# Block-sparse attention before a feed-forward layer: masked dense tiles replaced by gathered key and value blocks

## The chip, the cores and the metric

One NeuronCore of a Trainium2 chip runs the whole program. The metric is device time in microseconds (us), the median over the executions of a kernel. Engines are called PE (TensorE; PEld is its weight load), ACT (ScalarE), DVE (VectorE), POOL (GpSimd) and SP (SyncE, which here only issues DMA). PEclk is the clock that the throttle granted to TensorE, as a share of full speed. PV is the product of the exponentials with V; of the two operands of a matmul, the one that PEld loads is called stationary here, the other moving. A run is called slow when it took over 1.5% longer than the fastest of the same kernel, else fast; a single run alone is of unknown state. A call is a set of runs made together on one chip.

## The reference, cut to what matters

```python
# q, k, v: [4, 8, 768, 64] float32; blocks of 32 rows, 24 blocks; 3 sampled blocks a query block
mask = np.abs(blk_i - blk_j) <= 1                        # neighbours
mask = mask | (blk_i == 0) | (blk_j == 0) | (blk_i == 23) | (blk_j == 23)
for qb in range(24):
    for kb in sampled_blocks[qb]: mask[rows(qb), rows(kb)] = True
attn = softmax(where(mask, q @ k.T / 8, -1e9));  x = attn @ v   # -> [3072, 512]
h = x @ w_in                       # 512 -> 1024
solu = h * softmax(h)
out = layernorm(solu) * g_ln @ w_out                     # 1024 -> 512
```

A middle query block needs at most 8 of 24 key blocks: two ends, itself and two neighbours, three sampled.

## The kernel before: the parts that matter

It computes all 24 key blocks and adds the mask through extra contraction rows. Work goes by batch, query tile of 256 rows (`t`) and head pair. The three tiles of a batch are finished one after the other, so the feed-forward layer (FFN) of tile 0 starts after four short units, and one FFN tile is left over at the end.

```python
def transpose_pair(b, pr):                 # K and Q of two heads
    for src, dst in ((kc, kT[i]), (qc, qT[i])):
        tp = ps_m.tile([P, S], BF16, ...)  # PSUM
        for c in range(NCH):
            nc.tensor.matmul(tp[:, c*P:(c+1)*P], src[:, c, :, :], ident, is_transpose=True, ...)
        nc.vector.tensor_copy(out=dst[0:D, 0, pr, :], in_=tp[0:D, :])   # dense, L165
        nc.vector.tensor_copy(out=dst[D:P, 1, pr, :], in_=tp[D:P, :])   # dense, L166
# ... cut ...
units = [(b, t, pr) for b in range(B) for t in range(NT) for pr in range(NPR)]
for u, (b, t, pr) in enumerate(units):
    for n in range(3):
        scores(b, t, pr, n, exs)           # 4 matmuls of 256 columns, one Exp of 128x1024
        if n == 0 and prev is not None:
            pv(...)                        # 24 matmuls, 128 stationary columns, 65 moving
            if ppr == NPR - 1: bg.extend(ffn_pieces(...))
        if bg: bg.popleft()()              # one piece of an FFN tile between score groups
# in the FFN, the layer norm's row statistics run on POOL (L293 to L298 here):
#   mul, add, sub, pow(-0.5), each 128x2 or 128x4; the output scaling waits for the last
```

The softmax here doesn't subtract the row's maximum and nothing guards it: scores larger than these inputs give would overflow.

Of the kernel before, what the change touches and what calls it, by code (L numbers as in the profile page):

```python
# [10 lines left out]
I32 = mybir.dt.int32  # L11
AX = mybir.AxisListType
# [6 lines left out]
def kernel(  # L19
# [11 lines left out]
    nc = tc.nc  # L31
# [3 lines left out]
    NB = S // BLK  # L35
    NR = sampled_blocks.shape[1]
    P = 128
    NCH = S // P
    NT = 3
    TW = 2 * P  # L40
    NPR = H // 2
    NEG = -30000.0
# [8 lines left out]
    ld = ctx.enter_context(tc.tile_pool(name="ld", bufs=3))  # L51
    vpool = ctx.enter_context(tc.tile_pool(name="vpool", bufs=2))
    expp = ctx.enter_context(tc.tile_pool(name="expp", bufs=8))
# [6 lines left out]

    kT = [const.tile([P, 2, NPR, S], BF16, name=f"kT{i}") for i in range(2)]
    qT = [const.tile([P, 2, NPR, S], BF16, name=f"qT{i}") for i in range(2)]
    for t in (kT[0], qT[0]):
        nc.vector.memset(t[0:D, 1, 0, :], 0.0)
    va = [const.tile([P, H, NCH, D + 1], BF16, name=f"va{i}") for i in range(2)]


    def load_pair(b, pr):
        got = []
        for src, nm in ((k, "kc"), (q, "qc")):  # L70
            t = ld.tile([P, NCH, 2, D], BF16, tag=nm, name=nm)
            for hh in range(2):
                nc.gpsimd.dma_start(  # L73
                    out=t[:, :, hh, :],
                    in_=src[b, 2 * pr + hh, :, :].rearrange("(p c) d -> p c d", p=P))
            got.append(t)
        t = ld.tile([P, 2, NCH, D], BF16, tag="vc", name="vc")
        nc.gpsimd.dma_start(
            out=t.rearrange("p h c d -> p h (c d)"),
            in_=v[b, 2 * pr : 2 * pr + 2, :, :].rearrange("h (p c) d -> p h (c d)", p=P))  # L80
        got.append(t)
        return got

    loaded = {}
    loaded[(0, 0)] = load_pair(0, 0)


    ident = const.tile([P, P], BF16, name="ident")
    nc.vector.memset(ident, 0.0)
    nc.gpsimd.affine_select(out=ident, in_=ident, compare_op=ALU.not_equal,  # L90
                            fill=1.0, base=0, channel_multiplier=1,
                            pattern=[[-1, P]])

    maskT = const.tile([NB, NB], FP32, name="maskT")
    nc.vector.memset(maskT, 0.0)
    for base, cm, pat, fill in ((1, -1, [[1, NB]], NEG), (1, 1, [[-1, NB]], NEG),
                                (-1, 1, [[0, NB]], 0.0), (NB - 2, -1, [[0, NB]], 0.0),
                                (-1, 0, [[1, NB]], 0.0), (NB - 2, 0, [[-1, NB]], 0.0)):
        nc.gpsimd.affine_select(out=maskT, in_=maskT, compare_op=ALU.is_ge,
                                fill=fill, base=base, channel_multiplier=cm,  # L100
                                pattern=pat)
    _t = sampled_blocks.tensor
    _t32 = bass.DRamTensorHandle(_t.name, (2 * NB * NR,), I32)
    samp_i = const.tile([1, NB * NR, 2], I32, name="samp_i")
    nc.sync.dma_start(out=samp_i.rearrange("a b c -> a (b c)"),
                      in_=bass.AP(tensor=_t32, offset=0, ap=[[0, 1], [1, 2 * NB * NR]]))
    ones1 = const.tile([1, NB], BF16, name="ones1")
    nc.vector.memset(ones1, 1.0)
    samp_lo = const.tile([1, NB * NR], BF16, name="samp_lo")
    nc.vector.tensor_copy(out=samp_lo, in_=samp_i[:, :, 0])  # L110
    samp_ps = ps_m.tile([NB, NB, NR], FP32, tag="m", name="samp_ps")
    nc.tensor.matmul(samp_ps.rearrange("a b c -> a (b c)"), ones1, samp_lo,
                     start=True, stop=True)
    kb_iota_i = const.tile([NB, 1], I32, name="kb_iota_i")
    nc.gpsimd.iota(kb_iota_i, pattern=[[0, 1]], base=0, channel_multiplier=1)
    kb_iota = const.tile([NB, 1], FP32, name="kb_iota")
    nc.vector.tensor_copy(out=kb_iota, in_=kb_iota_i)
    eq = const.tile([NB, NB, NR], FP32, name="eq")
    nc.vector.tensor_scalar(out=eq, in0=samp_ps, scalar1=kb_iota, scalar2=None,
                            op0=ALU.is_equal)  # L120
    anyeq = const.tile([NB, NB], FP32, name="anyeq")
    nc.vector.tensor_reduce(out=anyeq, in_=eq, axis=AX.X, op=ALU.max)
    nc.vector.tensor_scalar(out=anyeq, in0=anyeq, scalar1=-1.0, scalar2=1.0,
                            op0=ALU.mult, op1=ALU.add)
    nc.vector.tensor_mul(out=maskT, in0=maskT, in1=anyeq)
    sel = const.tile([NB, NB, BLK], BF16, name="sel")
    nc.vector.memset(sel, 0.0)
    nc.gpsimd.affine_select(out=sel, in_=sel, compare_op=ALU.not_equal,
                            fill=1.0, base=0, channel_multiplier=1,
                            pattern=[[-1, NB], [0, BLK]])  # L130
    mskb = const.tile([NB, NB, BLK], BF16, name="mskb")
    nc.vector.tensor_copy(
        out=mskb, in_=maskT.rearrange("p (q o) -> p q o", o=1).broadcast_to([NB, NB, BLK]))

    selp = const.tile([NB, 1, S], BF16, name="selp")
    mskp = const.tile([NB, 1, S], BF16, name="mskp")
    for dst, src in ((selp, sel), (mskp, mskb)):
        nc.vector.tensor_copy(
            out=dst.rearrange("b o (c p) -> b (o c) p", c=NCH),
            in_=src.rearrange("b n o -> b (n o)").rearrange("b (p c) -> b c p", c=NCH))  # L140
# [3 lines left out]
    def put_mask_rows(i, p0, p1):  # L144
        for hh, r0 in ((0, D), (1, 0)):
            for dst, src in ((kT, selp), (qT, mskp)):
                for p in range(p0, p1):
                    nc.sync.dma_start(out=dst[i][r0 : r0 + NB, hh, p, :],
                                      in_=src[:, 0, :])

    for hh, r0 in ((0, D), (1, 0)):
        for dst, src in ((kT, selp), (qT, mskp)):
            nc.vector.tensor_copy(out=dst[0][r0 : r0 + NB, hh, 0, :], in_=src[:, 0, :])

    def transpose_pair(b, pr):
        i = b % 2
        kc, qc, vc = loaded.pop((b, pr))
        for src, dst in ((kc, kT[i]), (qc, qT[i])):
            tp = ps_m.tile([P, S], BF16, tag="m", name="tp")
            for c in range(NCH):  # L160
                nc.tensor.matmul(tp[:, c * P : (c + 1) * P],  # L161
                                 src[:, c, :, :], ident,
                                 is_transpose=True, start=(c == 0),
                                 stop=(c == NCH - 1))
            nc.vector.tensor_copy(out=dst[0:D, 0, pr, :], in_=tp[0:D, :])  # L165
            nc.vector.tensor_copy(out=dst[D:P, 1, pr, :], in_=tp[D:P, :])  # L166
        nc.vector.tensor_copy(out=va[i][:, 2 * pr : 2 * pr + 2, :, 0:D],
                              in_=vc)
# [3 lines left out]
    w_out_f = const.tile([P, KF, d_model], FP32, name="w_out_f")  # L172
    w_out_g = const.tile([P, KF, d_model], BF16, name="w_out_g")
# [5 lines left out]
    neg_half = const.tile([P, 2], FP32, name="neg_half")  # L179

    def load_weights():
        nc.gpsimd.dma_start(out=w_in_sb, in_=moe_w_in.rearrange("(c p) f -> p c f", p=P))
        nc.sync.dma_start(out=g_sb, in_=moe_g_ln.rearrange("(c p) -> p c", p=P))
        nc.sync.dma_start(out=w_out_f, in_=moe_w_out.rearrange("(c p) d -> p c d", p=P))
        nc.vector.memset(onesf, 1.0)
        nc.vector.memset(neg_half, -0.5)
        nc.vector.memset(st_sel, 1.0 / d_ff)
        nc.vector.memset(st_sel[:, :, 0:1], eps_ln ** 0.5)

    def prep_w1():  # L190
        for c in range(KF):
            nc.vector.tensor_scalar(out=w_out_g[:, c, :], in0=w_out_f[:, c, :],
                                    scalar1=g_sb[:, c : c + 1], scalar2=None,
                                    op0=ALU.mult)

    def prep_w2():
        cs = ps_m.tile([P, d_model], FP32, tag="m", name="cs")
        for c in range(KF):
            nc.tensor.matmul(cs, onesf, w_out_g[:, c, :], start=(c == 0),
                             stop=(c == KF - 1))  # L200
        nc.scalar.mul(out=wbar, in_=cs, mul=1.0 / d_ff)
        for c in range(KF):
            nc.vector.scalar_tensor_tensor(  # L203
                out=w_out_sb[:, c, :], in0=w_out_f[:, c, :], scalar=g_sb[:, c : c + 1],
# [3 lines left out]
    rows = (slice(0, D + NB), slice(0, P))  # L208

    def scores(b, t, pr, n, exs):  # L210
        i = b % 2
        s = ps_s.tile([P, 4, TW], FP32, tag="s", name="s")
        for m in range(4):
            hh, jc = divmod(4 * n + m, NCH)
            nc.tensor.matmul(s[:, m, :],  # L215
# [108 lines left out]
    for pr in range(1, NPR):  # L324
        loaded[(0, pr)] = load_pair(0, pr)
        if pr == 1:
            load_weights()
# [79 lines left out]
```

## Time and profile before

The median was 282.56 us (two runs, 282.11 to 283.0).

| | busy us | share |
|---|---|---|
| PE | 238.8 | 85% |
| ACT | 174.4 | 62% |
| DVE | 157.9 | 56% |
| POOL | 82.8 | 29% |

The page of the kernel before: busy time, DMA traffic, then the chain of work that ended last, by engine and by line.

```profile
span 281.1 us, 7445 instructions
...
PE 238.8 (85%) x3163; PEld 183.2 (65%) x3177; DVE 157.9 (56%) x365; ACT 174.4 (62%) x206; POOL 82.8 (29%) x142
...
DMA packets 61636, 20.40 MB, mean 73 GB/s; under 512 B 52225, under 2 KB 56994, under 8 KB 61602
...
PE 62%; DMA 11%; ACT 10%; DVE 9%; issue 3%; POOL 3%; ACTq 0%; POOLq 0%
```

PE is busy most of the span and is 62% of the chain: it is the bound.

The same kernel by stretches: until the first FFN matmul, until the last PV matmul, and the rest. Columns: the stretch, its length, busy us of PE, PEld, DVE, ACT and POOL (count), PEclk, DMA share and GB/s.

```profile
0.00:52.00 52.00, 24.09 (x242) 17.78 (x244) 34.41 (x79) 17.94 (x19) 34.28 (x53) 1.00 1.42 169
52.00:266.00 214.00, 205.52 (x2825) 159.42 (x2833) 117.18 (x274) 153.35 (x183) 47.24 (x85) 1.00 0.39 52
266.00:281.00 15.00, 9.17 (x99) 6.02 (x101) 6.27 (x13) 3.08 (x5) 1.27 (x4) 0.94 0.10 36
```

In the middle PE works 205.5 of 214 us at full clock.

The timeline of the kernel before, one burst of PV matmuls (start, length, engine, line, operation, count):

```profile
112.38 0.91 PE L231 MATMUL op<-va_92,ex 128*128 128x65 bf16 x24
```

### The profile page before, as it was taken

The numbers are of one execution on the slowest core, as the hardware profiler recorded it, in microseconds if no ns is written. First come the engines' busy times: TensorE is split into PE (matmuls) and PEld (weight loads), VectorE is DVE, ScalarE is ACT, GpSimd is POOL, SyncE is SP. The second block draws the span as 40 slices with busy tenths as digits, with TensorE's granted clock in tenths as the row PEclk, the third lists the DMA queues.
The fourth block names the chain that finished last, engine by engine and source line by source line (L and its number), as shares of the span: only waits on it lengthen the run. The fifth ranks groups of instructions, "written<-read, shape, count | busy, mean of one in ns | idle before, by whom it ended". The sixth has DMA issues, their size and how long they took to land.

```text
span 281.1 us, 7445 instructions
## 1 busy us (share of the span) xinstructions
PE 238.8 (85%) x3163; PEld 183.2 (65%) x3177; DVE 157.9 (56%) x365; ACT 174.4 (62%) x206; POOL 82.8 (29%) x142
## 2 busy tenths in 40 slices
PE   0116686999999999999999999999999999899783
PEld 0004564867867867867767768678678577686561
DVE  3079789648639622756666616386376236155261
ACT  1002468548858859667677688588488595785630
POOL 8695861218139110045253100140100101001001
PEclk9999999999999999999999999999999999999998
DMA  5999999409759810049279020090100200200202
GB/s 117 264 191 188 185 180 118 58 4 140 48 93 128 85 54 23 2 90 100 30 109 79 3 77 2 37 96 2 47 31 2 77 2 2 76 2 3 76 0 77
DMA packets 61636, 20.40 MB, mean 73 GB/s; under 512 B 52225, under 2 KB 56994, under 8 KB 61602
## 3 DMA queue, kind: packets, MB, share of 16 engines
q0 software_dynamic: 55056, 10.49, 45.8%
q1 hardware_dynamic: 6546, 9.43, 9.8%
q8 instruction: 25, 0.41, 0.6%
q14 instruction: 9, 0.07, 0.1%
HBM read 23.07 MB, written 6.29 MB: 104 GB/s over the span
## 4 chain that ended last, share of the span: by engine, by line
PE 62%; DMA 11%; ACT 10%; DVE 9%; issue 3%; POOL 3%; ACTq 0%; POOLq 0%
PE s L215 15%; PE h L268 15%; PE ops L304 14%; PE op L231 10%; ACT ex L220 8%; DMA kc<-in_k_dram 7%; PE s3p L283 6%; DMA vc<-in_v_dram 4%; DVE w_out_sb L203 2%; ACT ot L312 2%; PE tp L161 2%; POOL qc L73 1%; DVE xT L258 1%; PE tps L256 1%; DVE x L240 1%
## 5 line engine op out<-in xcount | busy, mean ns | idle before, releaser
L220 ACT ACTIVATE ex<-s 128x1024 bf16<-128x1024 f32 x144 | 141.1, 1024 | 68.9 <-PE s L215 67.8
L215 PE MATMUL s<-qT_87,kT_85 88*128 88x256 bf16 (+1 forms) x288 | 49.5, 284 | 5.8 <-ACT ex L220 3.1
L231 PEld LDWEIGHTS <-ex 128*128 128x128 bf16 x1152 | 45.7, 98 | 11.1 <-ACT ex L220 4.6
L268 PE MATMUL h<-xT,w_in_sb 128*128 128x256 bf16 x384 | 47.8, 272 | 1.3 <-DVE xT L258 0.6
L215 PE MATMUL s<-qT_88,kT_86 88*128 88x256 bf16 (+1 forms) x288 | 46.2, 272 | 2.0 <-ACT ex L220 1.2
L273 DVE TENSOR_TENSOR solu<-h,e 128x512 bf16<-128x512 f32 x48 | 33.0, 687 | 26.3 <-ACT e L272 26.2
L304 PE MATMUL ops<-w_out_sb,solu 128*128 128x512 bf16 x179 | 44.6, 378 | 0.9 <-DVE s_4734 L290 0.3
L268 PEld LDWEIGHTS <-w_in_sb 128*128 128x128 bf16 x384 | 37.0, 97 | 6.3 <-issue 1.6
L272 ACT ACTIVATE e<-h 128x512 bf16<-128x512 f32 x48 | 28.7, 598 | 18.1 <-PE h L268 16.9
L215 PEld LDWEIGHTS <-kT_85 88*128 88x128 bf16 (+1 forms) x288 | 27.3, 101 | 13.5 <-issue 6.0
L73 POOL DMA_DIRECT2D kc<-in_k_dram x32 | 26.8, 841 | 18.6 <-PE tp L161 17.7
L215 PEld LDWEIGHTS <-kT_86 88*128 88x128 bf16 (+1 forms) x288 | 26.0, 97 | 9.3 <-issue 4.0
L304 PEld LDWEIGHTS <-solu 128*128 128x128 bf16 x192 | 18.4, 97 | 18.1 <-issue 0.3
L73 POOL DMA_DIRECT2D qc<-in_q_dram x32 | 26.2, 822 | 8.0 <-DMA w_in_sb<-in_moe_w_in_dram 3.7
L231 PE MATMUL op<-va_92,ex 128*128 128x65 bf16 x576 | 26.2, 193 | 2.7 <-ACT ex L220 2.2
L231 PE MATMUL op<-va_91,ex 128*128 128x65 bf16 x576 | 25.2, 196 | 1.9 <-DVE x L240 1.0
L239 DVE RECIPROCAL r<-op 128x4 f32<-128x4 f32 x48 | 8.5, 180 | 30.8 <-PE op L231 29.3
L274 DVE TENSOR_TENSOR sq<-solu 128x512 bf16<-128x512 bf16 x48 | 20.4, 425 | 1.3
L240 DVE TENSOR_TENSOR x<-op,r 128x256 bf16<-128x256 f32 x48 | 20.1, 420 | 1.0
L161 PE MATMUL tp<-ident,kc 128*128 128x128 bf16 x96 | 9.2, 240 | 12.2 <-DMA kc<-in_k_dram 10.5
L309 DVE TENSOR_SCALAR ot<-ops,rs 128x512 f32<-128x512 f32 x12 | 9.0, 751 | 16.7 <-PE ops L304 12.7
L312 ACT ACTIVATE ot<-ops,rs 128x512 f32<-128x512 f32 x12 | 8.2, 687 | 14.3 <-PE ops L304 14.3
(127 smaller groups left out, 201.7 us busy)
## 6 DMA issues: line engine op xcount, KB each, us to landing
out_dram<-ot SPq DMA_DIRECT2D x24, 256.0 KB
kc<-in_k_dram POOLq DMA_DIRECT2D x32, 96.0 KB, 5.1
qc<-in_q_dram POOLq DMA_DIRECT2D x32, 96.0 KB, 4.4
vc<-in_v_dram POOLq DMA_DIRECT2D x16, 192.0 KB, 5.0
w_out_f<-in_moe_w_out_dram SPq DMA_DIRECT2D x1, 2048.0 KB
w_in_sb<-in_moe_w_in_dram POOLq DMA_DIRECT2D x1, 1024.0 KB, 9.5
kT_86<-selp SPq DMA_DIRECT2D x8, 36.0 KB
qT_88<-mskp SPq DMA_DIRECT2D x8, 36.0 KB
```

The costliest lines, as they stand in the source:

```text
L73: nc.gpsimd.dma_start(out=t[:, :, hh, :], in_=src[b, 2 * pr + hh, :, :].rearrange("(p c) d -> p c d", p=P))
L161: nc.tensor.matmul(tp[:, c * P : (c + 1) * P], src[:, c, :, :], ident, is_transpose=True, start=(c == 0), stop=(c == NCH - 1))
L215: nc.tensor.matmul(s[:, m, :], kT[i][rows[hh], hh, pr, jc * P : (jc + 1) * P], qT[i][rows[hh], hh, pr, t * TW : (t + 1) * TW], start=(m % ...
L220: nc.scalar.activation(out=e, in_=s, func=ACT.Exp, scale=scale)
L231: nc.tensor.matmul(op[:, qt, hh, :], exs[n][:, m, qt * P : (qt + 1) * P], va[i][:, 2 * pr + hh, jc, :], start=first, stop=(n == 2 and m == ...
L240: nc.vector.tensor_tensor(out=x[:, :, 2 * pr * D : (2 * pr + 2) * D].rearrange("p a (h d) -> p a h d", h=2), in0=op[:, :, :, 0:D], in1=r.b ...
L268: nc.tensor.matmul(h[:, ff, :], w_in_sb[:, c, f * P : (f + 1) * P], st["xT"][:, c, :], start=(ff == 0 and c == 0), stop=(ff == 1 and c == ...
L272: nc.scalar.activation(out=st["e"][:, sl, :], in_=h, func=ACT.Exp)
L273: nc.vector.tensor_mul(out=st["solu"][:, sl, :], in0=h, in1=st["e"][:, sl, :])
L274: nc.vector.tensor_mul(out=st["sq"][:, sl, :], in0=st["solu"][:, sl, :], in1=st["solu"][:, sl, :])
L283: nc.tensor.matmul(s3p[:, qt, g : g + 1], st[nm][:, f, qt * P : (qt + 1) * P], onesf[:, 0:1], start=first, stop=(qt == 1 and g == 2 and f ...
L304: nc.tensor.matmul(ops, st["solu"][:, f, qt * P : (qt + 1) * P], w_out_sb[:, f, :], start=(f == 0), stop=(f == KF - 1))
```

## The change

The intent is to compute only what the mask lets through. The scores of a head pair shrink from 9,216 PE columns to 3,584, and so does the exp on ACT. The price is data movement:

- K^T of a pair is copied to SBUF (`kT`); end and neighbour blocks are grouped by two DVE copies (`kg`); sampled blocks are gathered by POOL (`krt`, two indirect copies a pair).
- V is cast, written to a scratch in DRAM, read back in two layouts, and its sampled rows are gathered by 22 indirect DMAs a batch.
- Q^T is written block-diagonally (`qbd`), so that one matmul scores both heads.
- A unit is now a head pair over all 768 queries; the FFN of a batch starts after four pairs, and three FFN tiles of the last batch come at the end.

The core of the diff, cut:

```diff
-        nc.vector.tensor_copy(out=dst[0:D, 0, pr, :], in_=tp[0:D, :])
-        nc.vector.tensor_copy(out=dst[D:P, 1, pr, :], in_=tp[D:P, :])
+        tp = ps_m.tile([P, R8, PL], BF16, ...)          # R8 = 8 residues, PL = 96; key row = 8*a + r
+        for r in range(R8): nc.tensor.matmul(tp[:, r, :], kr[:, r, :, :], perm, is_transpose=True, ...)
+        nc.scalar.copy(out=kT.rearrange("p (a r) -> p r a", r=R8), in_=tp)              # L262
+        nc.vector.tensor_copy(out=kg[:, :, 1, :], in_=kT[:, 0 : NM * BLK]...)           # and ends, L266
+        for l in range(2):
+            nc.gpsimd.indirect_copy(krt[:, l*NL:(l+1)*NL, :], kT.bitcast(U32)..., kidx[:, l, 0:NLC], True)
+        for hh, eng in ((0, nc.scalar.copy), (1, nc.vector.tensor_copy)):               # L287
+            eng(out=dst[sl, :, hh, :].rearrange("p t (a r) -> p r t a", r=R8),
+                in_=tp[sl].rearrange("p r (t a) -> p r t a", t=NCH))
+    nc.sync.dma_start(out=v_s[b][0:S, :]..., in_=vst...)         # V round trip; v0, vn read back
+    nc.gpsimd.indirect_dma_start(out=t[:, i, :], in_=v_s[b][:, :], in_offset=...vidx...)   # 22 a batch
+    # scores: 17 matmuls of 128 columns and 22 of 64; PV: 64 or 32 stationary columns
-    units = [(b, t, pr) ...]
+    for n in range(N + 1):  b, pr = divmod(n, NPR)  ...
+        if i == 3 and ppr == NPR - 1:
+            for t in range(NT): bg.extend(ffn_pieces(pb, t, xs[pb]))
```

## The prediction

> **What bounds the kernel now.** TensorE. The page's busy table gives PE 239 of 281 us (85%), ACT 174, DVE 158, POOL 83; by stretches of 20 us, PE is 19.0 to 19.6 busy from 60 to 240 us, ACT only about 14.3. The chain of waits is 62% PE. One FFN tile is exposed at the end (about 266 to 279 us).
>
> From bursts in the timeline: a 256-column matmul costs about 107 ns, a 512-column one 214, a 128-column one 55, a 65-column PV matmul about 31. So PE needs: scores 576 x 107 = 62 us, PV 1152 x 31 = 36, FFN about 101 (h 41, ops 41, sums 13, transposes 5), K/Q transposes 11. Sum about 210.
>
> **What the change does.**
> - Scores: 147,456 columns become 57,344. Exp on ACT (144 x 1.02 = 141 us) falls to about 59. ACT gains the K^T and half of the Q^T copies, about 1.6 us a pair, 26 in all: 174 -> about 120.
> - PE scores: per pair 17 of 128 columns and 22 of 64, 1.65 us: 62 -> 26 us.
> - PV matmuls do not fall: 1152 -> 1248, now with 64 or 32 stationary columns. [...] Estimate 3.3 to 4.5 us a pair: 36 -> 53 to 72 us.
> - So PE is nearly unchanged: about 190 to 210 us. ACT was not the limit; most of its saving is worth nothing.
> - DVE: fp32 casts of K, Q, V and copies for grouped keys replace the transposed-tile copies. Estimate about 10 us a pair with FFN, 165 to 190 in all.
> - POOL: 32 indirect copies of 704 words and 88 indirect DMAs (a plain issue takes 0.82 us; I take 1.1). The copy's price is unknown[...]. I take 2.5. POOL total: 80 + 97 + 20, about 200 us.
>
> **The schedule.** V goes load, cast, DRAM, gather before the first PV: estimate PV of pair 0 at 35 to 48 us. Pairs 2 and 3 follow at about 9 us. FFN starts only after four pairs (about 66 us). Twelve pairs with three quarters of an FFN tile each cost PE about 12.6 us, 13.5 with waits: to about 228. Then three FFN tiles of the last batch are exposed instead of one, about 12 us each (the exposed tile before took about 13): 264 to 268.
>
> Prediction: 268 us, range 238 to 315. Faster by over 2%: 0.60; within: 0.13; slower: 0.27.
>
> **What would show it.** ACT busy about 120; score matmuls about 26 us of PE spacing; PV bursts of 24 narrow matmuls longer than the 0.91 us of 24 full ones; PE busy share lower than 85%; POOL about 200 with indirect copies near 2.5 us.
>
> **What would make it wrong.** Indirect copies at 5 us or gathers at over 1.5: POOL becomes the limit (over 17 us a pair), 300 to 340 us. Narrow PV matmuls as cheap as 31 ns or running side by side, and POOL out of the way: pairs of 11 us, about 240. A longer start (SP's in-order waits), or DVE lag stalling PE on the two-buffer PSUM pool, adds 10 to 30.

Two terms stay as my estimates, which no trace of the kernel before shows: 53 to 72 us of PE for PV, and 2.5 us for an indirect copy. The 5 us is a limit, not a measured price. PE is 26 + 53 to 72 + 101 + 11, about 190 to 210 us, and POOL is 80 (32 x 2.5) + 97 (88 x 1.1) + 20, about 200 us.

## More of the kernel before

DMA moves 20.4 MB.

The groups of instructions of the kernel before (by line; busy us, mean ns of one, then idle time before them and what ended it):

```profile
L220 ACT ACTIVATE ex<-s 128x1024 bf16<-128x1024 f32 x144 | 141.1, 1024 | 68.9 <-PE s L215 67.8
...
L166 DVE COPY kT_86<-tp 64x768 bf16<-64x768 bf16 x8 | 4.5, 561 | 0.1
```

The copy that takes a transposed tile out of PSUM costs 561 ns for 768 columns.

## The result and the profile after

The changed kernel took 464.07 us (463.91 and 464.22) against 282.56: 1.642 times the time, 95% interval 1.631 to 1.654. A ratio here is the mean time of one kernel's fast runs over that of the other's of the same rounds, so it is not quite the ratio of the medians. The output was correct. The prediction of 268 us, range 238 to 315, was wrong by far.

The page of the changed kernel:

```profile
span 462.1 us, 7827 instructions
...
PE 243.5 (53%) x3366; PEld 179.6 (39%) x3384; DVE 213.3 (46%) x362; ACT 201.3 (44%) x158; POOL 144.7 (31%) x181
...
DMA packets 35930, 52.86 MB, mean 114 GB/s; under 512 B 4276, under 2 KB 19256, under 8 KB 35896
...
ACT 23%; PE 21%; issue 17%; DVE 13%; POOL 12%; DMA 9%; another core or an unknown queue 3%; SPq 1%; ACTq 0%; POOLq 0%
ACT kT L262 10%; POOL vr L238 9%; PE h L441 7%; PE ops L477 4%; PE s L315 4%; ACT qbd_179 L287 4%; ACT qbd_180 L287 4%; DVE qbd_179 L287 3%; DVE qbd_180 L287 3%; DMA kc<-in_k_dram 3%; DMA v_240<-v_s_173 2%; PE op L354 2%; POOL krt L271 2%; PE s3p L456 2%
```

No engine is over 53% busy, and the chain is spread over all of them: the kernel is bound by waits. The copies `kT` and `qbd` out of the transposed tile are 24% of the chain (10+4+4+3+3). DMA moves 2.6 times the bytes.

Groups of the changed kernel:

```profile
L271 POOL INDIRECT_COPY krt<-kT,kidx 128x704 uint32 x32 | 40.7, 1273 | 184.4 <-issue 124.5
...
L262 ACT COPY kT<-tp 128x768 bf16<-128x768 bf16 x16 | 57.2, 3572 | 18.2 <-PE tp L259 18.2
...
L485 ACT ACTIVATE ot<-ops,rs 128x512 f32<-128x512 f32 x12 | 8.2, 687 | 96.4 <-POOL rs L471 27.5
...
L287 ACT COPY qbd_179<-tp 64x768 bf16<-64x768 bf16 x8 | 29.0, 3619 | 23.4 <-PE tp L282 23.4
L287 DVE COPY qbd_180<-tp 64x768 bf16<-64x768 bf16 x8 | 28.5, 3557 | 20.6 <-ACT qbd_180 L287 20.6
...
L482 DVE TENSOR_SCALAR ot<-ops,rs 128x512 f32<-128x512 f32 x12 | 9.0, 751 | 44.1 <-POOL rs L471 38.9
```

Each copy out of `tp` takes 3.56 to 3.62 us, where the kernel before took 0.56 for as many columns. On 16 pairs they are 57 us for `kT`, 58 for ACT's half of `qbd` and 57 for DVE's. The last number of DVE's `qbd` line says that DVE waited for ACT's half: the two halves run one after the other. The two `ot` lines are waits for POOL's `rs`, 27.5 and 38.9 us.

A stretch of the timeline of the changed kernel, one pair (lines of other engines left out; in brackets, idle time before and what ended it):

```profile
288.80 3.60 ACT L287 COPY qbd_180<-tp 64x768 bf16<-64x768 bf16 x1
...
292.42 3.55 DVE L287 COPY qbd_180<-tp 64x768 bf16<-64x768 bf16 x1 [0.70 <-ACT qbd_180 L287]
...
296.03 0.30 PE L456 MATMUL s3p<-onesf,e 128*128 128x1 bf16 x6 [4.69 <-DVE qbd_180 L287]
...
299.29 3.58 ACT L262 COPY kT<-tp 128x768 bf16<-128x768 bf16 x1
...
304.86 0.52 PE L354 MATMUL op<-vr,e_2813 128*32 128x65 bf16 x24
```

PE stands still for 4.69 us until DVE has finished the second half. The last line answers to the PV burst of before: 24 matmuls with 32 stationary columns take 0.52 us here, less than the 0.91 us of 24 full ones.

Another stretch, POOL alone:

```profile
226.16 1.70 POOL L271 INDIRECT_COPY krt<-kT,kidx 128x704 uint32 x1 [24.97 <-ACT e_2248 L321]
229.94 1.20 POOL L271 INDIRECT_COPY krt<-kT,kidx 128x704 uint32 x1 [2.08 <-issue]
231.30 1.29 POOL L238 DMA_INDIRECT vr<-v_s_175,vidx  x1 [0.17 <-issue]
232.90 0.96 POOL L238 DMA_INDIRECT vr<-v_s_175,vidx  x1 [0.30 <-issue]
...
245.44 0.95 POOL L238 DMA_INDIRECT vr<-v_s_175,vidx  x1 [0.30 <-issue]
246.41 0.21 POOL L466 TENSOR_TENSOR s_2228<-s_2226 128x4 f32<-128x4 f32 x1
...
247.24 0.73 POOL L471 TENSOR_TENSOR rs<-v_2230,neg_half 128x2 f32<-128x2 f32 x1
```

POOL took this work in the order shown. DVE had finished the input of the small statistics of an FFN tile (L466 to L471) at 226.2 us (L463); they started at 246.4, behind two indirect copies and a block of twelve gathers, one every 1.25 us. The output scaling (`ot`) waits for `rs`, and PE waits for the buffer that it frees. The lines of DVE and PE that end this wait:

```profile
248.00 0.75 DVE L482 TENSOR_SCALAR ot<-ops,rs 128x512 f32<-128x512 f32 x1 [10.41 <-POOL rs L471]
...
248.81 0.33 PE L354 MATMUL op<-v_389,e_1807 128*64 128x65 bf16 x4 [7.86 <-DVE ot L482]
```

PE stood idle for 7.86 us. The POOL lines also show an indirect copy's true price: its record is mostly 1.2 us (mean 1.27), but the second copy of a pair is preceded by at least 2.1 us with nothing to wait for that the profile shows, so that it starts 3.3 to 3.8 us after the first in most pairs.

The changed kernel by the same three stages:

```profile
0.00:143.00 143.00, 45.02 (x649) 36.31 (x650) 63.88 (x122) 62.47 (x36) 53.56 (x62) 0.61 0.71 169
143.00:421.00 278.00, 170.38 (x2418) 124.73 (x2428) 131.06 (x206) 129.61 (x107) 87.29 (x108) 0.73 0.38 97
421.00:462.00 41.00, 28.06 (x302) 18.58 (x307) 18.36 (x36) 9.23 (x15) 3.84 (x12) 0.96 0.14 46
```

All three stages are longer: 143 for 52, 278 for 214, 41 for 15. The granted clock is low in the first two (0.61 and 0.73), and PE's matmuls take longer at a low clock: the same `h` matmul took 327 ns in the second stage and 272 in the third, at a clock of 0.96; `ops` took 504 and 378.

### The profile page after: what moved, and what is told of

Its sections match the earlier page's. It is cut to its first block, busy times and chain, and to the rows that moved or that the text cites. A ratio compares the mean times of both kernels' runs of the same rounds, so it can differ in the third digit from the quotient of the medians.

```text
span 462.1 us, 7827 instructions
## 1 busy us (share of the span) xinstructions
PE 243.5 (53%) x3366; PEld 179.6 (39%) x3384; DVE 213.3 (46%) x362; ACT 201.3 (44%) x158; POOL 144.7 (31%) x181
## 2 busy tenths in 40 slices
DMA packets 35930, 52.86 MB, mean 114 GB/s; under 512 B 4276, under 2 KB 19256, under 8 KB 35896
## 4 chain that ended last, share of the span: by engine, by line
ACT 23%; PE 21%; issue 17%; DVE 13%; POOL 12%; DMA 9%; another core or an unknown queue 3%; SPq 1%; ACTq 0%; POOLq 0%
ACT kT L262 10%; POOL vr L238 9%; PE h L441 7%; PE ops L477 4%; PE s L315 4%; ACT qbd_179 L287 4%; ACT qbd_180 L287 4%; DVE qbd_179 L287 3%; DVE qbd_180 L287 3%; DMA kc<-in_k_dram 3%; DMA v_240<-v_s_173 2%; PE op L354 2%; POOL krt L271 2%; PE s3p L456 2%
## 5 line engine op out<-in xcount | busy, mean ns | idle before, releaser
L271 POOL INDIRECT_COPY krt<-kT,kidx 128x704 uint32 x32 | 40.7, 1273 | 184.4 <-issue 124.5
L477 PE MATMUL ops<-w_out_sb,solu 128*128 128x512 bf16 x174 | 58.9, 473 | 26.0 <-DVE qbd_180 L287 14.4
L441 PE MATMUL h<-xT,w_in_sb 128*128 128x256 bf16 x384 | 59.7, 313 | 23.3 <-DVE solu L446 21.3
L262 ACT COPY kT<-tp 128x768 bf16<-128x768 bf16 x16 | 57.2, 3572 | 18.2 <-PE tp L259 18.2
L445 ACT ACTIVATE e<-h 128x512 bf16<-128x512 f32 x48 | 31.2, 659 | 45.0 <-PE h L441 42.8
L485 ACT ACTIVATE ot<-ops,rs 128x512 f32<-128x512 f32 x12 | 8.2, 687 | 96.4 <-POOL rs L471 27.5
L287 ACT COPY qbd_179<-tp 64x768 bf16<-64x768 bf16 x8 | 29.0, 3619 | 23.4 <-PE tp L282 23.4
L287 DVE COPY qbd_180<-tp 64x768 bf16<-64x768 bf16 x8 | 28.5, 3557 | 20.6 <-ACT qbd_180 L287 20.6
L287 DVE COPY qbd_179<-tp 64x768 bf16<-64x768 bf16 x8 | 28.4, 3556 | 20.1 <-ACT qbd_179 L287 20.1
L287 ACT COPY qbd_180<-tp 64x768 bf16<-64x768 bf16 x8 | 28.6, 3571 | 6.9 <-PE tp L282 6.9
L264 DVE COPY kg<-kT 128x704 bf16<-128x704 bf16 x16 | 8.3, 520 | 49.1 <-ACT kT L262 49.1
L482 DVE TENSOR_SCALAR ot<-ops,rs 128x512 f32<-128x512 f32 x12 | 9.0, 751 | 44.1 <-POOL rs L471 38.9
L315 PEld LDWEIGHTS <-kg 128*128 128x128 bf16 x176 | 17.9, 136 | 29.0 <-issue 21.5
L238 POOL DMA_INDIRECT vr<-v_s_174,vidx x22 | 21.9, 993 | 19.1 <-DMA w_out_f<-in_moe_w_out_dram 8.9
L238 POOL DMA_INDIRECT vr<-v_s_175,vidx x22 | 21.4, 974 | 9.9 <-issue 6.1
L315 PEld LDWEIGHTS <-krt 128*128 128x128 bf16 x352 | 20.4, 120 | 8.7 <-issue 8.0
L238 POOL DMA_INDIRECT vr<-v_s_176,vidx x22 | 21.6, 983 | 5.9 <-issue 5.6
L238 POOL DMA_INDIRECT vr<-v_s_173,vidx x22 | 21.0, 953 | 6.6 <-issue 6.6
```

The costliest lines, as they stand in the source:

```text
L238: nc.gpsimd.indirect_dma_start(out=t[:, i, :], out_offset=None, in_=v_s[b][:, :], in_offset=bass.IndirectOffsetOnAxis(ap=vidx[:, qb : qb + ...
L262: nc.scalar.copy(out=kT.rearrange("p (a r) -> p r a", r=R8), in_=tp)
L271: nc.gpsimd.indirect_copy(krt[:, l * NL : (l + 1) * NL, :], kT.bitcast(U32).rearrange("p (b c) -> p b c", b=NB), kidx[:, l, 0:NLC], True)
L287: eng(out=dst[sl, :, hh, :].rearrange("p t (a r) -> p r t a", r=R8), in_=tp[sl].rearrange("p r (t a) -> p r t a", t=NCH))
L315: nc.tensor.matmul(s[:, o : o + w].rearrange("p (h c) -> p h c", h=2), lhsT, rhs, start=(o % 512 == 0), stop=((o + w) % 512 == 0 or j == i ...
L441: nc.tensor.matmul(h[:, ff, :], w_in_sb[:, c, f * P : (f + 1) * P], st["xT"][:, c, :], start=(ff == 0 and c == 0), stop=(ff == 1 and c == ...
```

## The experiments

Theory A: the strided copies are the main loss. Theory S: the FFN's statistics behind POOL's queue are a second. Theory B: the bytes of V's round trip hold up other loads. Rival to all: POOL's indirect copies and gathers alone set the pace. Ratios are of fast runs, against the kernel before on the same chip; a median may include a run of the slow state (one each in e3, e9, r14, r15 and r18, two each in e10 and e11; e5 is one run of unknown state). "Stages" are start, middle and tail in us, as above.

| run | kernel | us | ratio | stages |
|---|---|---|---|---|
| e1_dense_writes | dense copies | 379.29 | 1.343 | 116, 219, 42 |
| e2_rs_on_dve | statistics on DVE | 443.24 | 1.571 | 143, 254, 45 |
| e3_both | both | 354.34 | 1.254 | 114, 192, 45 |
| e4_pool_idle | both, POOL nearly idle (wrong) | 306.57 | 1.087 | 106, 156, 45 |
| e5_two_per_line | probe of the copy | 388.05 | – | – |
| e6_kq_on_act | e3, K/Q loads on ACT's queue | 387.65 | 1.378 | 120, 220, 45 |
| e7_v_staged_once | e4, V staged once (wrong) | 288.17 | 1.023 | 94, 149, 45 |
| e8_interleaved_ffn | e6, FFN tiles side by side | 378.1 | 1.339 | 121, 220, 36 |
| e9_e3_interleaved | e3, FFN tiles side by side | 370.93 | 1.308 | 114, 220, 36 |
| e10_ends_on_chip | e9, end rows of V spread on chip | 367.18 | 1.297 | 119, 218, 36 |
| e11_e7_interleaved | e7, FFN tiles side by side (wrong) | 277.57 | 0.986 | 92, 144, 36 |
| e12_last_batch_only | e3, only the last batch side by side | 372.55 | 1.323 | 116, 219, 36 |
| r13_after_again | the changed kernel | 463.78 | 1.634 | 142, 278, 42 |
| r14_e3_again | e3 | 351.46 | 1.240 | 114, 189, 45 |
| r15_e6_again | e6 | 357.9 | 1.259 | 112, 199, 43 |
| r16_e12_again | e12 | 345.91 | 1.219 | 114, 194, 36 |
| r17_e4_again | e4 | 307.33 | 1.090 | 108, 155, 43 |
| r18_e7_again | e7 | 285.91 | 1.013 | 93, 148, 42 |

Runs e1 to e4 shared one chip, e5 to e8 a second, e9 and e10 a third, e11 and e12 a fourth, r13 to r16 a fifth, r17 and r18 a sixth. This turned out to matter.

### e1: the copies written densely

```diff
-        nc.scalar.copy(out=kT.rearrange("p (a r) -> p r a", r=R8), in_=tp)
+        nc.scalar.copy(out=kT.rearrange("p (a r) -> p a r", r=R8), in_=tp.rearrange("p r a -> p a r"))
# and the same exchange of loops in both qbd copies
```

> The three copies out of the transposed PSUM tile (K^T on ACT, half of Q^T on ACT, half on DVE) write SBUF densely and read PSUM with a stride instead; nothing else changes, the result stays right. Theory A (the 3.57 us copies, 48 of them, cause the loss: their 16-byte write stride, about 4.6 ns an element): each falls to 0.8 to 1.2 us, and since K's copy, Q's first and Q's second copy follow one another in each pair, about 16 x 8 = 128 us go: 320 to 350 us. Rival B (the POOL queue sets the pace: indirect copies, then a block of gathers, then the small FFN statistics behind them): the copies get short but the time stays over 420 us. Rival C: the copies are slow because of the transposed order itself, and stay over 3 us when the read is strided: 450 to 475 us.

It took 379.29 us (377.45 to 379.69), output correct: 85 us less than 464. The same elements are moved; only the order differs, so that the SBUF side is now contiguous and the PSUM side strided. Groups of this version:

```profile
L262 ACT COPY kT<-tp 128x768 bf16<-128x768 bf16 x16 | 12.8, 797 | 19.7 <-PE tp L259 19.3 <-PE s L315 0.4
L287 ACT COPY qbd<-tp 64x768 bf16<-64x768 bf16 x16 | 12.6, 788 | 33.1 <-PE tp L282 33.1
...
L287 DVE COPY qbd<-tp 64x768 bf16<-64x768 bf16 x16 | 15.4, 961 | 5.8 <-ACT qbd L287 5.4
```

From 3.57 us to 0.80 and 0.96. DVE's copy of 768 columns that was dense on both sides took 0.56 in the kernel before, so this form, strided on the PSUM side, took 0.40 us more. Theory A holds as the largest single term. It explains less than I expected (320 to 350 us).

### e2 and e3: the statistics moved to DVE, alone and with e1

```diff
-            nc.gpsimd.tensor_mul(out=s2, ...)   # and add, sub
-            nc.gpsimd.tensor_tensor(out=rs, in0=v2, in1=neg_half, op=ALU.pow)
+            nc.vector.tensor_mul(out=s2, ...)   # and add, sub; then the inverse square root by
+            # a shift of the float's bits and two Newton steps, all 128x2 on DVE
```

> The slow copies stay; the four small FFN statistics operations leave POOL for DVE (inverse square root by a shift and two Newton steps, result right), so that they no longer wait behind indirect copies and gathers. Theory A: at most 15 us faster, 449 to 470 us. Rival B (POOL queue): the waits of ot for rs (38.9 us on DVE, 27.5 us on ACT in the waits view) go, 390 to 430 us.

> Dense writes and the statistics on DVE together, result right. If A and B both hold and add: about 290 to 310 us. If only A holds: the same as e1 within 10 us. If only B holds: the same as e2 within 10 us.

e2 took 443.24 us (441.88 to 444.18), 21 us less than 464; e3 took 354.34 (351.37 to 356.82), 25 us less than e1. Both outputs are correct. The two repairs add up: 85 + 21 = 106 of the measured 110. Theory S holds as a second term, but both times fell between the ranges that I had written down: e2 gained more than the 15 us of one theory and less than the 34 to 74 of the other, and e3 missed the 290 to 310 us of "both add" since e1 and e2 had each gained less than expected. Twelve FFN tiles with four tiny operations each had looked like nothing: about 1.3 us of busy time a tile, but in the wrong queue.

### e4: POOL nearly idle

```diff
# wrong on purpose: V gathered only for batch 0, indirect copies only for pair 0
     def gather_v(b, g):
+        if b > 0: vr[(b, g)] = vr[(0, g)]; return
-        for l in range(2):
+        for l in range(2 if n == 0 else 0):
```

> Wrong on purpose: as e3, but gathers only for the first batch and indirect copies only for the first pair, their results used throughout. It bounds what POOL still costs after e3. If POOL (indirect copies 3.3 us start to start, gathers 1.25 us) still paces the kernel: 30 us or more below e3, 250 to 270 us. If PE, DVE and the exposed start and end pace it: within 15 us of e3.

306.57 us (two runs): 48 less than e3, more than the 30 expected of a POOL that still costs time, though above the 250 to 270 us written down. This takes away POOL's time and also the gathers' traffic (44.06 MB for 52.86), and the two are not told apart. The remainder, still 25 us above the kernel before, is not POOL's. The rival that POOL alone sets the pace falls, also because e1 gained 85 us with POOL's work untouched.

### e5: how many elements must share 16 bytes

```diff
-        nc.scalar.copy(out=kT.rearrange("p (a r) -> p a r", r=R8), in_=tp.rearrange("p r a -> p a r"))
+        nc.scalar.copy(out=kT.rearrange("p (a s w) -> p s a w", s=4, w=2), in_=tp.rearrange("p (s w) a -> p s a w", w=2))
# and four neighbours (w=4) in the qbd copies
```

> Only a probe of the copies: the changed kernel with its loop order changed so that two neighbouring elements (K^T copy) or four (Q^T copies) are written into each 16-byte line before the next line. Theory A [...]: the K^T copy of 768 columns falls from 3.57 us to 0.8 to 1.0 us already with two, and Q's with four to the same. Rival (the cost is a fixed time for each line visited): K^T about 1.8 us with two, Q about 0.9 to 1.0 with four. Rival (any non-unit write step stops the fast path): all stay near 3.5 us.

The copies of this version, K^T with two neighbours and Q^T (`qbd`) with four:

```profile
L288 DVE COPY qbd<-tp 64x768 bf16<-64x768 bf16 x16 | 15.4, 960 | 8.8 <-ACT qbd L288 4.3 <-issue 4.2
...
L262 ACT COPY kT<-tp 128x768 bf16<-128x768 bf16 x16 | 13.7, 859 | 18.6 <-PE tp L259 17.8 <-ACT e L322 0.8
...
L288 ACT COPY qbd<-tp 64x768 bf16<-64x768 bf16 x16 | 12.6, 788 | 36.8 <-remote 28.1 <-PE tp L283 8.8
```

Two neighbours per 16 bytes give 0.86 us, four give 0.79 (ACT) and 0.96 (DVE), eight gave 0.79 to 0.80 (ACT) and 0.96 (DVE), one gave 3.56 to 3.62. A fixed price for each visit to 16 bytes would have made two neighbours cost about half of 3.57. Theory A's times (0.8 to 1.0 us already with two) came out. For these bf16 writes the price of one alone is (3572 - 797) ns over 768 columns, 3.6 ns an element on ACT, and (3557 - 961), 3.4 ns, on DVE.

What it is about the lone element stays open, for two neighbours also fill a 4-byte word. Two small DVE casts in the setup of the changed kernel speak for this rival:

```profile
L131 DVE CAST blk<-u_i 128x24 f32<-128x24 int32 x1 | 0.2, 178 | 0.0
L110 DVE CAST q_f<-q_i 128x24 f32<-128x24 int32 x1 | 0.2, 173 | 0.1
```

L131 writes 24 lone fp32 values 16 bytes apart, L110 writes 24 densely. At 3.4 ns an element L131 would take 81 ns longer; it took 5. No run tested more than these 24 elements, or two bf16 that share 16 bytes without being neighbours. Reads were not hit like this either: the kernel before reads 768 bf16 of SBUF 12 bytes apart in 0.65 us (L138).

### e6 and e7: SP's queue, and V's round trip

```diff
# e6: K and Q loads off SP
-            nc.sync.dma_start(out=t..., in_=src...)
+            nc.scalar.dma_start(out=t..., in_=src...)
# e7 (on e4; wrong on purpose): V of batch 0 serves all batches
     def load_v(b, i):
+        if b > 0: return
     def stage_v(b):
+        if b > 0: vt[b] = vt[0]; return
```

> e3 with the K and Q loads issued from ACT's queue, so that they no longer stand in SP's queue behind the V write that waits for a cast and for landings. Theory D (head-of-line blocking in SP's queue lengthens the start): the first FFN matmul, at 114 us in e3, comes 15 to 30 us earlier, total 325 to 342 us. Rival E (the start is bound by the bytes that the 16 DMA engines move, 160 to 300 GB/s there): under 8 us change, 347 to 360 us.

> Wrong on purpose: as e4_pool_idle, and V is loaded, cast, written to DRAM and spread out only for the first batch. Rival E (bytes of the V round trip): the first FFN matmul (105.7 us in e4) comes 15 us or more earlier and the total falls by 20 to 40 us, to 265 to 287. If the bytes do not matter: 298 to 307 us.

The waits that e6's expectation means are in e3's trace: SP's write of V to DRAM waited up to 20.9 us at a time for DVE, and the read back 12.3 us, in four waits, for the write to land.

e6 took 387.65 us, apparently 33 more than e3, and its first PV came at 62.2 us instead of 43.8. e7 took 288.17, apparently 18 less than e4. Both comparisons cross from one chip to another. r15, r17 and r18 below redo them.

### e8 to e12: the exposed FFN tiles

```diff
-                    for t in range(NT):
-                        bg.extend(ffn_pieces(pb, t, xs[pb]))
+                    f = [ffn_pieces(pb, t, xs[pb]) for t in range(NT)]
+                    bg.extend(f[0][0:5])
+                    for t in range(1, NT):   # the end of tile t-1 among the steps of tile t
+                        bg.extend([f[t][0], f[t][1], f[t-1][5], f[t][2], f[t-1][6], f[t][3], f[t-1][7], f[t][4]])
+                    bg.extend(f[NT - 1][5:8])
# e10 also: end rows of V read once by DMA and spread over 11 groups by a DVE copy
# e12: only where pb is the last batch
```

> e6 with the three FFN tiles of a batch emitted interleaved (the statistics and output of one between the matmuls of the next). The exposed end after the last PV (45 us in e3) should fall to 30 to 36 us: 8 to 15 us under e6. If the end is limited by PE work alone (about 8.4 us a tile, 25 us) plus its two-buffer PSUM evictions, less than 4 us change.

> The version with dense copies and statistics on VectorE (354.34 us) with its feed-forward tiles emitted stage by stage, several tiles side by side, as in the run that did so on the other base and gained 9.5 us. Theory T (the exposed feed-forward tiles at the end are latency chains, so side by side they overlap): 340 to 350 us, the tail after the last PV 36 us instead of 45. Rival (the end is bound by throughput or the order only pushes work elsewhere): within 3 us of 354, tail unchanged. None of the theories puts it under the kernel before (282).

> The run beside it with one change: the V rows of the first and last key blocks are read from HBM once and spread over the eleven groups by a VectorE copy, instead of eleven times by DMA (about 2.9 MB less of DMA traffic; a right result). Theory B (the bytes of the V round trip hold up the loads of K and Q, so the start of the chain): 5 to 12 us below its neighbour, the first PV and the first feed-forward matmul both earlier. Rival (bytes of V do not matter, only the indices' latency and the queue on POOL do): within 3 us, or slower by the cost of the added VectorE copies.

> The wrong-on-purpose version whose gathers and V staging happen only once (288.17 us), with its feed-forward tiles emitted side by side. The same edit cost 16 us where POOL was busy: the middle grew by 28 us, the tail shrank by 9. Theory Q (the middle grew because POOL's copies and gathers come out later when attention's steps stand behind more feed-forward work, and POOL has no slack): with POOL idle the middle stays within 5 us of 149 and the whole falls to 277 to 284 us. Rival R (the order itself stalls TensorE, ScalarE or VectorE, whatever POOL does): the middle grows by 15 us or more and the whole is above 292.

> The version with dense copies and statistics on VectorE (354.34 us, a right result), with only the last batch's three feed-forward tiles side by side. Nothing else is left to be delayed by them, so both Q and R expect the start and middle unchanged (114 and 192) and the tail 36 us instead of 45: 342 to 350 us. If the middle grows all the same, or the tail does not shrink, the reading of the tail as a latency chain falls. Not expected to reach the kernel before (282).

e8 gained 9.5 us over e6 on the same chip, all of it in the tail (36 for 45 us). e9, the same edit on e3, came out at 370.93, above e3 instead of below: a miss. Its tail had shrunk to 36, but its middle was 220 instead of 192. I formed theory Q, that the mixed order starved POOL. e11 seemed to bear it out: with POOL idle the edit gave 277.57, inside the expected 277 to 284. e12 then broke theory Q. In e12 every engine has the same order of instructions as e3 until the last batch's FFN. Yet its middle took 219 us too. An edit in the tail can't lengthen the middle, so the difference had to come from elsewhere: the chip or the call.

e10 was 3.8 us below its neighbour e9 with overlapping intervals (1.289 to 1.306 against 1.298 to 1.318), and two of its five runs were slow, the profiled one among them. The first PV did come 4.1 us earlier (38.7 for 42.8). As a gain in time it is unclear.

### r13 to r18: the same kernels beside each other

These change nothing but the chip.

> The changed kernel itself, once more, beside the three others of this call on one chip. Theory C (a chip, or the call, moves these DMA-bound kernels by some per cent though it does not move the kernel before): it may stand 3 to 6% off 464. Rival N (times hold from call to call): 460 to 468.

> The version with dense copies and statistics on VectorE, unchanged (354.34 us in the first call). The last run of the last call had the same order of instructions on every engine up to the last batch's feed-forward tiles, and yet its middle took 220 us instead of 192. Theory C: this run takes 370 to 380 us here with a middle near 220, or the next-but-one run falls back to 342 to 350; the two agree within 12 us on one chip. Rival (something in the tail's emission does change the middle): this run 352 to 357, the other 370 or more.

> The version with K and Q loads on ScalarE's queue (387.65 us in another call, so compared across calls with 354.34). Theory C: its distance from the run beside it shrinks from 33 us to 5 to 18. Rival (the loads on another queue do cost that much, by taking DMA from the V round trip: first PV at 62 instead of 44 us): 25 us or more above the run beside it; the first PV at 60 to 64 us either way.

> The version with only the last batch's feed-forward tiles side by side (372.55 us in the last call). On one chip with its parent: theory C (tail shorter, the rest equal): 6 to 12 us below the parent of this call. Rival: 15 us or more above it, with the middle longer by 28 us again.

On one chip: the changed kernel 463.78, e3 351.46, e6 357.9, e12 345.91. So e12 is 5 to 6 us below its parent (I had expected 6 to 12), and moving the K/Q loads costs 5 to 6 us, not 33 (fast runs alone), though the first PV still comes at 62.6 us against 43.5. Theory D of e6 falls: the first FFN matmul came 2 us earlier (111.6 for 113.8), not 15 to 30. Of e12's tail gain of 9 us part is missing because the middle of its profiled run was 194 us and that of e3's 189. Theory C holds for e6 and e12, not for the changed kernel itself, which came back within 0.1% (that these kernels are DMA-bound, as r13's expectation has it, was not shown; the DMA share in the middle of e12 was 0.48 and 0.54): the same program e12 took 372.55 on one chip and 345.91 on another, and e6 387.65 and 357.9, while the kernel before stayed within 0.5% in its medians (281.5 to 282.9).

The two executions of the identical program, first on the slower chip:

```profile
116.00:334.00 218.00, 154.78 (x2419) 110.20 (x2419) 122.02 (x320) 76.92 (x107) 81.50 (x76) 0.80 0.48 124
```

and e12 again on the other (stretches: middle and tail):

```profile
114.00:308.00 194.00, 148.12 (x2430) 104.95 (x2428) 135.79 (x320) 76.32 (x107) 83.75 (x76) 0.87 0.54 141
308.00:344.00 36.00, 27.37 (x316) 19.20 (x312) 23.85 (x77) 9.12 (x15) 0.00 (x0) 0.95 0.15 52
```

On the slower chip ACT's and POOL's busy time is the same within 3%, PE's is 4.5% longer and DVE's 10% shorter, but the work is spread over 218 instead of 194 us with DMA at 124 instead of 141 GB/s. What differs in the chip, or in that call, stays open. Only comparisons on one chip are used from here on, apart from the changed kernel's first run, which repeated. For the same reason the middle of e9 is left unexplained, and e11's gain over e7 is not a clean measurement: they ran on different chips.

> The wrong-on-purpose version with gathers for the first batch only and indirect copies for the first pair only (306.57 us in the first call), now on one chip with the version that also stages V only once. Theory B (the V round trip's bytes delay the loads of K and Q even with POOL idle): 10 us or more above its neighbour. Rival (the 18 us between them came from different chips): within 5 us of its neighbour.

> The version that also stages V only once (288.17 us on another chip). With fewer bytes it should be the less dependent on the chip: 283 to 292 us, 10 to 22 us below its neighbour under theory B, within 5 under the rival. The stages 94, 149, 45 us should come back within 4 us each.

On one chip e4 took 307.33 and e7 285.91: 21.4 us for V's repeated staging (44.06 MB against 30.16). So staging V repeatedly costs this much, which is what theory B expected. But e7 drops V's loads, DVE casts and waits in SP's queue along with the bytes, so that the bytes alone are the cause is not shown; e10, which took away 2.7 MB only, was unclear. e7 again, by stages:

```profile
0.00:94.00 94.00, 35.69 (x648) 30.01 (x650) 46.61 (x122) 29.39 (x36) 26.52 (x37) 0.78 0.79 199
94.00:238.00 144.00, 127.62 (x2369) 97.41 (x2379) 108.32 (x310) 75.35 (x106) 0.00 (x0) 0.99 0.21 64
238.00:283.00 45.00, 30.07 (x353) 19.90 (x357) 26.60 (x82) 9.92 (x16) 0.00 (x0) 0.99 0.14 47
```

Here is what is left of the sparsity's gain. With copies dense, POOL idle and V staged once, the middle takes about 148 us where the kernel before needs 214. But the start takes 93 instead of 52 and the tail about 42 instead of 15 (the printed cut at 238 lies a little before the last PV at 240.6). The middle is 66 us shorter, start and tail together are 68 us longer, so even this unreal version stands at 1.013. The 66 us are not all saved work: before, the middle holds eleven FFN tiles and the PV of 44 of 48 short units; after, nine tiles and the PV of 12 of 16 pairs. The rest moved to the start and the tail. Over the whole span PE's busy time fell by 45 us (238.8 to 193.4).

## Why the prediction was wrong, point by point

The loss can be added up with the runs (medians; the last step is taken from r17 and r18 on one chip):

| step | us | removed |
|---|---|---|
| changed kernel | 464 | |
| e1: dense copies | 379 | 85 |
| e3: statistics off POOL | 354 | 25 |
| e4: POOL's copies and gathers with their traffic | 307 | 48 |
| e7 (r18): V staged once | 286 | 21 |
| before | 282 | |

- **The step that failed first.** The prediction said: "ACT gains the K^T and half of the Q^T copies, about 1.6 us a pair, 26 in all". The form was right, the term mis-sized: 3.57 + 3.6 = 7.2 us a pair on ACT, 115 us in all, and 3.56 a pair on DVE. I had priced the copies by columns from the kernel before and not looked at the output's stride of 16 bytes in the diff. With dense copies a pair costs ACT 0.80 + 0.79 us, the "about 1.6" predicted, and ACT is 115.4 us busy, the "about 120" predicted. This term made 85 us of the 182 lost (e1); the points below are the rest. Together they took the pace from PE: the pairs of the middle, "about 12.6 us, 13.5 with waits" in the prediction, took 23.2 (278 us for twelve), with PE busy 14.2 of them.
- **"POOL total: 80 + 97 + 20, about 200 us"** counted only a total, and it was less than the span. What hurt was the order. Twelve gathers in one block at 1.25 us are 15 us, and the FFN's statistics stand behind them. Moving those alone gave 21 to 25 us. The prices themselves were nearer: 1.25 us for a gather (predicted 1.1), 3.3 to 3.8 us from copy to copy (predicted 2.5). The 2.5 was my estimate: the kernel before has no indirect copy to take it from. What POOL's copies and gathers still cost after that, 48 us with their traffic, is not split further.
- **The bytes were not in the prediction at all**; V's round trip stood there only as a delay before the first PV. 52.86 MB against 20.40 MB: staging V for every batch cost 21 us with POOL idle, bytes, casts and queue together.
- **"FFN starts only after four pairs (about 66 us)"**: it started at 143 us, at 116 with dense copies (114 in e3), and at 93 in e7 run again (r18). "PV of pair 0 at 35 to 48 us" was right (44.0). So the four pairs, not the first PV, were mis-sized. At 199 GB/s and a DMA share of 0.79 the start of e7 is mostly transfers; that these bound it was argued, not tested.
- **The tail** was right in size: three exposed tiles "about 12 us each" against 41 to 45 us. Side by side they take 36.
- **Narrow PV matmuls.** "Estimate 3.3 to 4.5 us a pair" was wrong the other way. It was my estimate, and no trace had shown narrow matmuls to be dearer. Bursts of 24 narrow matmuls take 0.37 to 0.52 us in the changed kernel, with the records of their weight loads (0.24 to 0.36 us) in the same stretch, against 0.91 for full ones. A pair's 44 narrow and 34 half-width ones come to an estimated 1.8 to 2.5 us, worked out from those bursts and from twelve half-width ones in 0.38 to 0.54 us.
- **"PE is nearly unchanged"** came out (243.5 busy for 238.8), but by luck, for a reason I had not given: the saved score columns were offset by slower matmuls at a lower granted clock (0.71 in the mean of the profiled run; the FFN's `h` matmuls took 313 ns for 272, `ops` 473 for 378). The "190 to 210" was summed from spacings, which gave 210 for the kernel before, where the page says 238.8 busy; so the 193 us that PE is busy in e7 run again (r18), at a mean clock of 0.92, do not confirm it.

No version beats the kernel before with a right result. The best, e12 in r16, takes 345.91 us (1.219).

## What to carry to other kernels

Read the output access pattern of every added copy, not only its element count: writes that land one bf16 in each 16 bytes of SBUF cost 4.5 times as much on ScalarE (3.57 us for 0.80, 768 columns) and 3.7 times on VectorE (3.56 for 0.96) here, and swapping two loops removed that with no other change. Before counting saved work as a gain, follow what stands in front of what in a shared queue (small operations stood 20 us behind copies and gathers on POOL; moving them gave 21 to 25) and the ends of the schedule: here the coarser unit of work lengthened the start (93 us for 52) and the tail (42 for 15) even where the middle was a third shorter (148 for 214), part of it because work had moved out of it. And compare versions on the same chip: two of these versions full of short waits moved by 27 to 30 us between chips or calls, while the PE-bound kernel before did not.
